# Turning values and phi(keys) to token layout by VectorE's 32x32 blocks and a DMA round trip instead of TensorE

## The chip, the cores and the metric

The kernel runs on one core of one Trainium2 chip. A core has a matrix engine (TensorE, PE in the profile, with its weight loads as PEld), a vector engine (VectorE, DVE), a scalar engine (ScalarE, ACT), GpSimd (POOL) and a sync engine (SyncE, SP) that here only issues DMAs. [...] The metric is the device time of one execution in microseconds; a comparison uses the median of several.

## The reference: one transformer block

The input x has 2048 tokens of 1024 features. The block computes h = x + A(layernorm(x)) and then h2 = h + B(layernorm(h)). B is an MLP: a dense layer to 3584 features, gelu, a dense layer back. A is attention with a compressive memory: 32 heads of 32 features; the tokens are taken in four segments of 512, and a memory M and a normaliser z are carried from one to the next:

```python
phi = lambda t: jnp.where(t > 0, t + 1.0, jnp.exp(t))
for s in range(N):
    logits = einsum("bhqd,bhkd->bhqk", qs, ks) * scale + mask
    a_dot = einsum("bhqk,bhkd->bhqd", softmax(logits), vs)
    a_mem = einsum("bhld,bhde->bhle", phi(qs), M) / (phi(qs) . z + 1e-6)
    outs.append(g * a_mem + (1 - g) * a_dot)
    M = M + einsum("bhld,bhle->bhde", phi(ks), vs)
    z = z + sum over tokens of phi(ks)
```

Two products sum over tokens: the attention product with vs and the memory update of phi(ks) with vs. TensorE sums over the partition axis, so both need vs (and the second phi(ks)) with tokens on partitions. All values are float32; the kernel splits each operand into an upper half that TensorE's fast format holds exactly and a lower half (the rest), and adds three products: upper-upper, upper-lower, lower-upper.

## The kernel before: units, slots and queues

The 2048 tokens are done in two halves of two segments each. In a half come the attention, the output projection (wo) and the MLP; the second half ends with the second MLP layer for all tokens. The change is in `attention`.

**Units.** Attention works on 8 groups of 4 heads (128 features) by 2 segments of the half: 16 units in a half, 32 in all. `dense(g, sl, ws, u)` (L402) makes a unit's operands: the projections of keys, queries and values in this order (`project`, 24 matmuls of 128x512 each, a yield after every third), into accumulators kps, qps, vps with features on partitions and 512 tokens along the row. Keys and queries are split (kh, kl, qh, ql) and copied by DMA into stacks of 96 partitions per head (`stack`, L372: twelve DMAs of 64 KB on SP's queue for the keys, twelve for the queries; five stack buffers for keys and five for queries). For segments 0 to 2, phi of the keys (pk) is made in the query projection's step 2 by `phi_sum`.

**Turning, before.** In step 1 of the value projection four TensorE transposes (L453) write pk in token layout to the accumulator pkn. ScalarE copies the upper half (pkh, L455), and in step 2 VectorE subtracts the lower (pkl, L457). After the value projection ScalarE copies vps to SBUF (vt, L461). The turn of the values is put off to the next unit: `late` (L466), a generator that the next unit's `dense` steps from the key projection's step 2 on. It issues four TensorE transposes (L469) to vn, the upper half by ScalarE (vs, L471) and the lower half by VectorE (L472). vs holds sixteen blocks of 64 columns (upper 32, lower 32), block 4 x (token block) + head. Then `late` queues the memory products (pm, segments 1 to 3: twelve matmuls) and the memory update (pmm, segments 0 to 2: twelve matmuls), which `one_small` hands out one by one between other TensorE work.

**Slots.** Beside the projections of a unit run the heads of the unit before (`heads`, `slot`): per head, scores (qk, L541), a maximum and exponential (L542, L550), a normalisation on GpSimd (L557), ten transposes of the weights (ptr, L573) with copies by ScalarE (pth, L575) and VectorE (ptl, L580), and the attention products with vs (av, L593), which come two head slots after the scores. `interleave` steps projections and slots in turn, six steps for a head, in the order PLAN (L31).

**What sets the order.** The text gives priorities; the framework plans each engine's and each DMA queue's order from them and from what it takes to be ready. Outside attention most of the text is pinned by `in_order`. An engine and a queue then run strictly in the planned order. Accumulators of tag "d" (three of 128x512) are shared by kps, qps, vps, pkn, vn, pm, pmm, pom and the output projection.

**The end of a half.** The last unit's heads run beside the first blocks of the output projection (`wo_first`, L729). Its fourth weight block lives in the tile pair that `zx_tile(x_, 3)` gives (tags th3 and tl3, one buffer each): `more` in L732.

Of the kernel before, what the change touches and what calls it, by code (L numbers as in the profile page):

```python
# [17 lines left out]
P = 128  # L18
# [25 lines left out]
def build(tc, x, wq, wk, wv, wo, beta, w1, b1, w2, b2, out):  # L44
# [6 lines left out]
    def ps_dense(name):  # L51
        return psum.tile([P, 512], F32, tag="d", name=name, bufs=3)
# [29 lines left out]
    p1_dram = [dram.tile([P, 512], F32, name=f"p1_dram{j}") for j in range(FB // 2)]  # L82
    h_dram = [[dram.tile([S // P, P, FB // 4, P], F32, name=f"h_dram{i}{s}") for s in range(2)] for i in range(2)]

    acts = {}

    def split(pool, w, hi, lo, hi_eng="vector", lo_eng="gpsimd"):
# [256 lines left out]
    def attention(half, first):  # L344
# [4 lines left out]
        def tmp(name):  # L349
            return ab.tile([P, 512], F32, tag="tmp", name=name, bufs=5)  # L350

        def tmpr(name):
            return ab.tile([P, 512], F32R, tag="tmpr", name=name, bufs=6)

# [12 lines left out]
        def phi_sum(parts, name, acc=None):  # L367
            o = tmp(name)
            nc.vector.scalar_tensor_tensor(o, parts[0], 1.0, parts[1], op0=ALU.min, op1=ALU.add, accum_out=acc)
            return o  # L370
# [31 lines left out]
        def dense(g, sl, ws, u):  # L402
# [15 lines left out]
            for c in project(ws["q"], sl, "qps", qps):  # L418
                if c == 0:
                    u["ks"] = stack(kh, kl, "ks", (0, 1, 0))  # L420
                if c == 2 and s < 3:
                    zc = ab.tile([P, 64], F32, name="zc", bufs=2)[:, 0:1]
                    pk = phi_sum(kparts, "pk", zc)
                next(behind, None)
                yield
            qh, ql = tmpr("qh"), tmpr("ql")
# [6 lines left out]
            for c in project(ws["v"], sl, "vps", vps):  # L433
                if c == 0:
                    u["qs"] = stack(qh, ql, "qs", (0, 0, 1))
                if s > 0:
                    if c == 2:
                        pq = phi_sum(qparts, "pq")
                    if c == 4:
                        while small:  # L440
                            one_small()
                        pqh, pql = tmpr("pqh"), tmpr("pql")
                        mzh = ab.tile([P, 256], F32R, name="mzh", bufs=1)[:, 0:132]
                        mzl = ab.tile([P, 256], F32R, name="mzl", bufs=1)[:, 0:132]
                        nc.scalar.copy(pqh, pq)
                        nc.gpsimd.tensor_copy(mzh, MZ[:, g, :])
                        nc.gpsimd.tensor_tensor(mzl, MZ[:, g, :], raw(mzh), op=ALU.subtract)
                    if c == 5:
                        nc.gpsimd.tensor_tensor(pql, pq, raw(pqh), op=ALU.subtract)
                if c == 1 and s < 3:  # L450
                    pkn = ps_dense("pkn")
                    for i in range(4):
                        nc.tensor.transpose(pkn[:, i * P:(i + 1) * P], pk[:, i * P:(i + 1) * P], ident)  # L453
                    pkh, pkl = tmpr("pkh"), tmpr("pkl")
                    nc.scalar.copy(pkh, pkn)  # L455
                if c == 2 and s < 3:
                    nc.vector.tensor_tensor(pkl, pkn, raw(pkh), op=ALU.subtract)  # L457
                next(behind, None)
                yield
            vt = tmp("vt")  # L460
            nc.scalar.copy(vt, vps)  # L461
            vs = ab.tile([P, 16, 64], F32R, name="vs", bufs=2)
            u["vs"] = vs
            omt = u["omt"] = tmp("omt") if s > 0 else None

            def late():  # L466
                vn = ps_dense("vn")
                for c in range(4):
                    nc.tensor.transpose(vn[:, c * P:(c + 1) * P], vt[:, c * P:(c + 1) * P], ident)  # L469
                vn3 = vn.rearrange("p (a b) -> p a b", b=DH)  # L470
                nc.scalar.copy(vs[:, :, 0:32], vn3)  # L471
                nc.vector.tensor_tensor(vs[:, :, 32:64], vn3, raw(vs[:, :, 0:32]), op=ALU.subtract)  # L472
                yield
                if s > 0:
                    om = tmp("om")
# [19 lines left out]
                if s < 3:  # L495
                    def update(pmm):
                        nc.vector.tensor_tensor(MZ[:, g, 0:P], pmm[:, 0:P], MZ[:, g, 0:P], op=ALU.add)  # L497
                        own = MZ[:, g, 0:P].rearrange("p (h e) -> p h e", h=4)
                        nc.gpsimd.tensor_tensor(own, own, hsel.unsqueeze(2).to_broadcast([P, 4, DH]), op=ALU.mult)
                        z = ZC[:, g:g + 1]  # L500
                        nc.gpsimd.tensor_scalar(z, z, zc, None, op0=ALU.add)
                        nc.gpsimd.tensor_scalar(MZ[:, g, 128:132], hsel, z, None, op0=ALU.mult)

                    smalls("pmm", [(lambda ps: ps[:, 0:P].rearrange("p (a b) -> p a b", a=4),
                                    pkh[:, c * P:(c + 1) * P], pkl[:, c * P:(c + 1) * P],
                                    vs[:, 4 * c:4 * c + 4, 0:32], vs[:, 4 * c:4 * c + 4, 32:64], c == 0, c == 3)
                                   for c in range(4)], update)
                total = len(small)
                while len(small) > total - left:
# [72 lines left out]
        def av(st, n):  # L582
# [3 lines left out]
            po = st["po"]  # L586
            for jk in (0, 1) if n == 0 else (3, 2):
                w = 512 - P * jk
                v = u["vs"][:, 4 * jk + j, :]
                for part in ("pth", "ptl"):  # L590
                    if (jk, part) != (3, "ptl"):
                        one_small()
# [851 lines left out]
```

## Time and profile before

| | us |
|---|---|
| timed runs, median of 3 | 2302.25 (2301.9 to 2303.4) |
| span of the profiled execution | 2296.2 |
| TensorE busy | 2270.4 |
| VectorE busy | 1540.3 |
| ScalarE busy | 1225.0 |
| GpSimd busy | 1092.4 |

The span runs from the first to the last instruction of one profiled execution; a timed run also holds what lies around it, so the two differ by some 6 us. Matmuls are pipelined: two that follow each other overlap in the records, and the distance between their starts tells what one costs. In the rows of the prediction "SPq" is an issue on SP's DMA queue, and a DMA row gives the median time from issue to landing. Row groups show busy time, the mean of one in ns, and the idle time of the engine just before them.

### The profile page before, as it was taken

What the parts mean: (1) busy time and instruction counts of PE and PEld (TensorE: products, weight loads), DVE (VectorE), ACT (ScalarE), POOL (GpSimd) and SP (SyncE); (2) the same over time, 40 slices, a digit from 0 to 9 for tenths busy, and PEclk for the clock granted to TensorE, in tenths of its full rate; (3) what the DMA queues carried; (4) which work ended last, traced back from release to release, by engine and by line L of the source; (5) the groups of instructions that cost most, each with busy time, mean ns of one, the idle gap of its engine ahead of it and who ended that gap; (6) DMA issues with size and microseconds to landing.
All of it is one profiled execution on the core that took longest, in us unless ns stands there. A gap on an engine that the chain in (4) does not pass through costs nothing.

```text
span 2296.2 us, 35279 instructions
## 1 busy us (share of the span) xinstructions
PE 2270.4 (99%) x11769; PEld 1890.8 (82%) x11769; DVE 1540.3 (67%) x3173; ACT 1225.0 (53%) x2549; POOL 1092.4 (48%) x1134
## 2 busy tenths in 40 slices
PE   8999999999999999999999999999999999999999
PEld 6888888878888888888888887888888888888887
DVE  6777777776655565777777777565566766577563
ACT  6777777775453445777777776363344223322221
POOL 5545555555244442555555556253445554155430
PEclk9999999999999999999999999999999999999999
DMA  6333333345465654433333344466667976476762
GB/s 190 92 85 91 93 89 85 87 120 182 139 204 172 188 165 142 113 91 86 85 87 88 87 111 140 156 211 175 176 188 263 345 243 216 159 253 221 249 234 90
DMA packets 322719, 355.36 MB, mean 155 GB/s; under 512 B 26190, under 2 KB 218730, under 8 KB 322538
## 3 DMA queue, kind: packets, MB, share of 16 engines
q1 hardware_dynamic: 259370, 316.40, 45.4%
q10 hardware_dynamic: 63168, 36.71, 5.3%
q8 instruction: 93, 1.52, 0.3%
q14 instruction: 88, 0.72, 0.1%
HBM read 226.59 MB, written 76.09 MB: 132 GB/s over the span
## 4 chain that ended last, share of the span: by engine, by line
PE 91%; ACT 3%; POOL 2%; DVE 2%; issue 1%; DMA 1%; ACTq 0%; SPq 0%; POOLq 0%; DVEq 0%
PE po L1278 22%; PE bps L882 9%; PE cps L882 7%; PE dps L882 6%; PE po L593 6%; PE ppt L573 6%; PE pqk L541 3%; PE vps L116 2%; PE vps L115 2%; PE kps L115 2%; PE kps L116 2%; PE vps L117 2%; PE kps L117 2%; PE pwo L117 2%; PE pwo L116 2%; PE pwo L115 2%
## 5 line engine op out<-in xcount | busy, mean ns | idle before, releaser
L557 POOL TENSOR_SCALAR pr<-pr,nm,gate 128x128 f32<-128x128 f32 (+3 forms) x512 | 322.6, 639 | 345.9 <-DVE nm L554 260.0
L550 ACT ACTIVATE pr<-pr,mx 128x256 f32<-128x256 f32 (+3 forms) x512 | 287.6, 562 | 161.9 <-DVE mx L542 158.2
L580 DVE TENSOR_TENSOR ptl<-ppt,pth 128x512 fp32r<-128x512 f32 (+1 forms) x384 | 227.2, 599 | 86.2 <-ACT pth L575 82.0
L542 DVE CUSTOM_DVE_ANT_0 pr<-pqk,mask 128x256 f32<-128x256 f32 (+3 forms) x512 | 243.3, 484 | 46.5 <-PE pqk L541 43.7
L573 PE MATMUL ppt<-ident,pr 128*128 128x128 f32 x1280 | 223.6, 277 | 2.1 <-POOL pr L557 1.4
L575 ACT CAST pth<-ppt 128x512 fp32r<-128x512 f32 (+1 forms) x384 | 194.2, 517 | 39.0 <-PE ppt L573 33.1
L1288 DVE TENSOR_TENSOR c<-c,po 128x512 f32<-128x512 f32 x160 | 105.4, 683 | 143.1 <-PE po L1278 135.5
L573 PEld LDWEIGHTS ppt<-ident,pr 128*128 128x128 f32 x1280 | 164.6, 140 | 32.5 <-POOL pr L557 2.6
L541 PE MATMUL pqk<-ks,qs 96*128 96x256 f32 (+3 forms) x512 | 161.3, 315 | 0.0
L92 POOL TENSOR_TENSOR wl<-wr,wh 128x1024 fp32r<-128x1024 f32 x52 | 124.5, 2393 | 70.8 <-PE pqk L541 27.6
L593 PE MATMUL po<-pth,vs 128*64 128x512 f32 (+3 forms) x512 | 155.4, 326 | 0.3 <-ACT pth L575 0.2
L593 PE MATMUL po<-ptl,vs 128*64 128x512 f32 (+3 forms) x512 | 153.9, 310 | 1.3 <-DVE ptl L580 1.2
L1278 PE MATMUL po<-w2h,zh 128*128 128x512 f32 x378 | 121.1, 390 | 0.8 <-DVE zh L1218 0.4
L1135 POOL TENSOR_TENSOR w2r<-w2r 128x512 f32<-128x512 f32 x54 | 85.4, 1593 | 72.0 <-DVE c L1288 36.9
L541 PEld LDWEIGHTS pqk<-ks,qs 96*128 96x128 f32 x512 | 96.2, 188 | 21.5
L994 POOL TENSOR_TENSOR s<-r 128x512 f32<-128x512 f32 x28 | 43.6, 1559 | 143.4 <-DVE sa L1010 87.1
L882 PE MATMUL bps<-zh,sb 128*128 128x512 f32 x336 | 111.0, 391 | 0.0
L882 PE MATMUL bps<-zh,sa 128*128 128x512 f32 x336 | 110.8, 390 | 0.0
L115 PE MATMUL vps<-yh,wh 128*128 128x512 f32 x256 | 109.4, 427 | 0.9 <-DVE MZ L497 0.9
L115 PE MATMUL kps<-yh,wh 128*128 128x512 f32 (+1 forms) x264 | 110.1, 417 | 0.0
L115 PE MATMUL qps<-yh,wh 128*128 128x512 f32 x256 | 106.8, 417 | 0.0
L1278 PE MATMUL po<-w2h,hl 128*128 128x512 f32 x322 | 103.2, 390 | 0.5 <-POOL hl L1218 0.3
(241 smaller groups left out, 6657.1 us busy)
## 6 DMA issues: line engine op xcount, KB each, us to landing
hr<-h_dram SPq DMA_DIRECT2D x112, 448.0 KB, 5.4
w2r<-in_B_w SPq DMA_DIRECT2D x122, 256.0 KB, 4.4
r<-in_B_w SPq DMA_DIRECT2D x56, 512.0 KB, 4.5
h_dram<-ht ACTq DMA_DIRECT2D x84, 256.0 KB, 3.7
ks<-kh SPq DMA_DIRECT2D x256, 64.0 KB, 2.0
qs<-qh SPq DMA_DIRECT2D x256, 64.0 KB, 2.0
wr<-in_A_wo SPq DMA_DIRECT2D x32, 512.0 KB, 4.0
wx<-in_B_w SPq DMA_DIRECT2D x56, 256.0 KB, 3.5
```

The costliest lines, as they stand in the source:

```text
L115: nc.tensor.matmul(ps, ah, bh, start=first, stop=False)
L116: nc.tensor.matmul(ps, ah, bl, start=False, stop=False)
L541: nc.tensor.matmul(pqk[:, :n], u["qs"][j][:, i * P:(i + 1) * P], u["ks"][j][:, 0:n], start=True, stop=True)
L542: nc.vector.tensor_tensor_reduce(out=st["pr"][:, offs[i]:offs[i] + n], in0=pqk[:, :n], in1=mask[:, 512 - n:512], op0=ALU.add, op1=ALU.min, ...
L550: nc.scalar.activation(pi, pi, AF.Exp, bias=mx[:, i:i + 1], scale=-1.0, accum_out=mx[:, 4 + i:5 + i])
L557: nc.gpsimd.tensor_scalar(pi, pi, nm[:, 4 + k:5 + k], gate[:, 1, 4 * g + j:4 * g + j + 1], op0=ALU.mult, op1=ALU.mult)
L573: nc.tensor.transpose(ppt[:, o:o + P], pr[:, offs[i] + jk * P:offs[i] + (jk + 1) * P], ident)
L575: acts["pth"] = n, nc.scalar.copy(pth[:, base:base + w], ppt[:, :w])
L580: nc.vector.tensor_tensor(o, x0, x1, op=ALU.subtract)
L593: nc.tensor.matmul(po[:, P * jk:], v, st[part][:, koff[jk]:koff[jk] + w], start=(jk, part) == (0, "pth"), stop=(jk, part) == (2, "ptl"))
L882: nc.tensor.matmul(ps, x_[:, c, :], y_[:, c, :], start=first and c == 0 and n == 0, stop=last and c == 3 and n == 2, skip_group_check=True)
L1278: nc.tensor.matmul(ps, x_[:, k], y_[k], start=opens and k == 0 and i == 0, stop=closes and k == self.KP - 1 and i == 2, skip_group_check=True)
```

## The change

A helper `turned(src, to, at)` turns a [128 features, 512 tokens] tile without TensorE. VectorE transposes 32x32 blocks into `mid`, with block columns reordered on the way; a DMA stores `mid` to DRAM; four DMAs read it back, each for one of four sets of 32 partitions, so that tokens lie on partitions. All five are issued by SP, and the reads follow the store. The result is ordered by head and then by token block, so the users' indices change (block 4 x head + token block). `turned` is called for pk in the query projection's step 3, and for vps, straight from the accumulator, at the end of the value projection; the copy vt, the eight transposes and the accumulators pkn and vn go. The upper halves are still copied by ScalarE, now from SBUF (that of the keys one step later), and the lower halves are subtracted by GpSimd instead of VectorE. `mid` and the result are quarters of two scratch tiles `scr` with the tags th3 and tl3, taken at the start of `attention`.

```diff
@@ -82,6 +82,7 @@
     p1_dram = [dram.tile([P, 512], F32, name=f"p1_dram{j}") for j in range(FB // 2)]
     h_dram = [[dram.tile([S // P, P, FB // 4, P], F32, name=f"h_dram{i}{s}") for s in range(2)] for i in range(2)]
 
+    turn_dram = [dram.tile([P, 512], F32, name=f"turn_dram{k}") for k in range(4)]
     acts = {}
 
     def split(pool, w, hi, lo, hi_eng="vector", lo_eng="gpsimd"):
@@ -349,6 +350,19 @@
         def tmp(name):
             return ab.tile([P, 512], F32, tag="tmp", name=name, bufs=5)
 
+        scr = [acts["zt"].tile([P, 4, 512], F32, tag=f"t{x_}3", name=f"sc{x_}") for x_ in "hl"]
+
+        def turned(src, to, at):
+
+            mid = at
+            nc.vector.transpose(mid.rearrange("p (c k d) -> p c k d", c=4, k=4), src.rearrange("p (k c d) -> p c k d", c=4, k=4))
+            d = turn_dram[acts.get("turned", 0) % len(turn_dram)]
+            acts["turned"] = acts.get("turned", 0) + 1
+            nc.sync.dma_start(d, mid)
+            for c in range(4):
+                nc.sync.dma_start(to[32 * c:32 * c + 32].rearrange("j (h x) -> j h x", h=4),
+                                  d[:, c * P:(c + 1) * P].rearrange("(h j) x -> j h x", h=4))
+
         def tmpr(name):
             return ab.tile([P, 512], F32R, tag="tmpr", name=name, bufs=6)
 
@@ -421,6 +435,9 @@
                 if c == 2 and s < 3:
                     zc = ab.tile([P, 64], F32, name="zc", bufs=2)[:, 0:1]
                     pk = phi_sum(kparts, "pk", zc)
+                if c == 3 and s < 3:
+                    kn = scr[1][:, 2 + sl]
+                    turned(pk, kn, scr[1][:, sl])
                 next(behind, None)
                 yield
             qh, ql = tmpr("qh"), tmpr("ql")
@@ -447,29 +464,26 @@
                         nc.gpsimd.tensor_tensor(mzl, MZ[:, g, :], raw(mzh), op=ALU.subtract)
                     if c == 5:
                         nc.gpsimd.tensor_tensor(pql, pq, raw(pqh), op=ALU.subtract)
-                if c == 1 and s < 3:
-                    pkn = ps_dense("pkn")
-                    for i in range(4):
-                        nc.tensor.transpose(pkn[:, i * P:(i + 1) * P], pk[:, i * P:(i + 1) * P], ident)
+                if c == 2 and s < 3:
                     pkh, pkl = tmpr("pkh"), tmpr("pkl")
-                    nc.scalar.copy(pkh, pkn)
-                if c == 2 and s < 3:
-                    nc.vector.tensor_tensor(pkl, pkn, raw(pkh), op=ALU.subtract)
+                    pkn = kn.rearrange("p (h k d) -> p k h d", h=4, k=4)
+                    pk4 = [x_.rearrange("p (k h d) -> p k h d", h=4, k=4) for x_ in (pkh, pkl)]
+                    nc.scalar.copy(pk4[0], pkn)
+                if c == 3 and s < 3:
+                    nc.gpsimd.tensor_tensor(pk4[1], pkn, raw(pk4[0]), op=ALU.subtract)
                 next(behind, None)
                 yield
-            vt = tmp("vt")
-            nc.scalar.copy(vt, vps)
+            vn = scr[0][:, 2 + sl]
+            turned(vps, vn, scr[0][:, sl])
             vs = ab.tile([P, 16, 64], F32R, name="vs", bufs=2)
             u["vs"] = vs
             omt = u["omt"] = tmp("omt") if s > 0 else None
 
             def late():
-                vn = ps_dense("vn")
-                for c in range(4):
-                    nc.tensor.transpose(vn[:, c * P:(c + 1) * P], vt[:, c * P:(c + 1) * P], ident)
                 vn3 = vn.rearrange("p (a b) -> p a b", b=DH)
                 nc.scalar.copy(vs[:, :, 0:32], vn3)
-                nc.vector.tensor_tensor(vs[:, :, 32:64], vn3, raw(vs[:, :, 0:32]), op=ALU.subtract)
+                nc.gpsimd.tensor_tensor(vs[:, :, 32:64], vn3, raw(vs[:, :, 0:32]), op=ALU.subtract)
+                vk = vs.rearrange("p (h k) e -> p k h e", h=4)
                 yield
                 if s > 0:
                     om = tmp("om")
@@ -503,7 +517,7 @@
 
                     smalls("pmm", [(lambda ps: ps[:, 0:P].rearrange("p (a b) -> p a b", a=4),
                                     pkh[:, c * P:(c + 1) * P], pkl[:, c * P:(c + 1) * P],
-                                    vs[:, 4 * c:4 * c + 4, 0:32], vs[:, 4 * c:4 * c + 4, 32:64], c == 0, c == 3)
+                                    vk[:, c, :, 0:32], vk[:, c, :, 32:64], c == 0, c == 3)
                                    for c in range(4)], update)
                 total = len(small)
                 while len(small) > total - left:
@@ -586,7 +600,7 @@
             po = st["po"]
             for jk in (0, 1) if n == 0 else (3, 2):
                 w = 512 - P * jk
-                v = u["vs"][:, 4 * jk + j, :]
+                v = u["vs"][:, 4 * j + jk, :]
                 for part in ("pth", "ptl"):
                     if (jk, part) != (3, "ptl"):
                         one_small()
```

## The prediction

> **What bounds the kernel now.** I read the page's head and its chain first, then the busy time of two attention stretches (the view by windows; only its sum row is shown), then TensorE in order of time.
>
> ```profile
> span 2296.2 us, 35279 instructions
> PE 2270.4 (99%) x11769; PEld 1890.8 (82%) x11769; DVE 1540.3 (67%) x3173; ACT 1225.0 (53%) x2549; POOL 1092.4 (48%) x1134
> PE 91%; ACT 3%; POOL 2%; DVE 2%; issue 1%; DMA 1%; ACTq 0%; SPq 0%; POOLq 0%; DVEq 0%
> sum 870.00, PE 866.72 PEld 732.20 DVE 653.16 ACT 637.50 POOL 469.87; mean PE 433.36 PEld 366.10 DVE 326.58 ACT 318.75 POOL 234.93
> ```
>
> TensorE carries 91% of the chain, and in the two attention stretches (870 us) it is busy 866.72 us, with VectorE at 75%, ScalarE at 73% and GpSimd at 54%. So TensorE time removed there shortens the kernel, as long as nothing new makes TensorE wait. How much a transpose costs is read from starts, not from durations:
>
> ```profile
> 213.46 0.39 PE L117 MATMUL vps<-yh,wl 128*128 128x512 f32 x1
> 213.69 0.60 PE L453 MATMUL pkn<-ident,pk 128*128 128x128 f32 x4
> 214.12 0.38 PE L573 MATMUL ppt<-ident,pr 128*128 128x128 f32 x2
> ...
> 217.41 0.34 PE L541 MATMUL pqk<-ks,qs 96*128 96x384 f32 x1
> 217.59 0.60 PE L573 MATMUL ppt<-ident,pr 128*128 128x128 f32 x4
> ...
> 220.91 0.39 PE L117 MATMUL vps<-yh,wl 128*128 128x512 f32 x1
> ...
> 224.44 0.60 PE L469 MATMUL vn<-ident,vt 128*128 128x128 f32 x4
> 224.79 0.43 PE L541 MATMUL pqk<-ks,qs 96*128 96x384 f32 x1
> 225.06 0.60 PE L573 MATMUL ppt<-ident,pr 128*128 128x128 f32 x4
> ...
> 227.48 0.22 PE L395 MATMUL pmm<-vs,pkh 128*128 128x128 f32 x1
> ```
>
> Columns: start, duration, engine. Four key transposes hold the next work back by 214.12 - 213.69 = 0.43 us. Four value transposes take 224.79 - 224.44 = 0.35 us, and the score matmul behind them needs 0.27 us to its successor instead of the 0.18 us at 217.41: together 0.44 us.
>
> **The change, part by part.** Counts and durations by line:
>
> ```profile
> L453 PE MATMUL pkn<-ident,pk 128*128 128x128 f32 x96 | 14.4, 272 | 0.0
> L469 PE MATMUL vn<-ident,vt 128*128 128x128 f32 x128 | 19.3, 273 | 0.6 <-ACT vt L461 0.6
> L461 ACT COPY vt<-vps 128x512 f32<-128x512 f32 x32 | 18.9, 592 | 1.0 <-PE vps L117 0.9
> L472 DVE TENSOR_TENSOR vs<-vn,vs 128x512 fp32r<-128x512 f32 x32 | 22.0, 686 | 0.7 <-ACT vs L471 0.4 <-DMA qs<-qh 0.3
> L369 DVE SCALAR_TENSOR_TENSOR pk<-e,r 128x512 f32<-128x512 f32 x24 | 21.5, 894 | 20.4 <-ACT r L364 20.4
> L449 POOL TENSOR_TENSOR pql<-pq,pqh 128x512 fp32r<-128x512 f32 x24 | 31.0, 1290 | 27.4 <-ACT pqh L445 26.1 <-DMA qs<-ql 1.3
> ```
>
> *TensorE removed:* 24 key turns (96 / 4) x 0.43 us and 32 value turns (128 / 4) x 0.44 us = 10.3 + 14.1 = **24.4 us**. This is the gain's ceiling.
>
> [...]
>
> *ScalarE:* the copy of L461 goes (18.9 us in all, not on the path, counted as nothing). The upper halves of L455 and L471 stay, now read from on-chip memory instead of the accumulators.
>
> *VectorE:* 56 subtractions go (L472 and its twin L457, 0.69 us each) and 56 block transposes of 128x512 come. No row shows such a transpose. A one-pass 128x512 operation costs between the 0.69 us of L472 and the 0.89 us of L369; I take 0.69 and a balance of nothing. At 0.89 it would be 11 us more over an engine that is idle a quarter of the time, hidden. If it were half as fast as that, some 40 us; still hidden in sum, but late by 0.7 us each time.
>
> *GpSimd:* 56 subtractions of 128x512 at the 1.29 us of L449 = 72 us more, 1.3 us per turn. In the two stretches it is idle 400 of 870 us, so the sum is covered; the place in its queue is the third rival.
>
> *DMAs:* each turn adds five issues to SP's queue, a 256 KB store and, behind a wait for its landing, four 64 KB reads. The rows for them and for SP's queue now:
>
> ```profile
> ks<-kh SPq DMA_DIRECT2D x256, 64.0 KB, 2.0
> o_dram<-ot SPq DMA_DIRECT2D x28, 256.0 KB, 2.3
> orr<-o_dram SPq DMA_DIRECT2D x28, 256.0 KB, 3.2
> ```
> ```profile
> 220.89 0.59 SPq L377 DMA_DIRECT2D qs<-ql  x1
> 231.99 0.51 SPq L377 DMA_DIRECT2D ks<-kh  x1
> ```
> ```profile
> 237.65 0.59 SPq L377 DMA_DIRECT2D ks<-kh  x1
> ...
> 243.83 1.17 SPq L377 DMA_DIRECT2D qs<-qh  x2
> ...
> 250.74 0.59 SPq L377 DMA_DIRECT2D qs<-ql  x1
> ```
> ```profile
> 233.84 0.70 DVE L369 SCALAR_TENSOR_TENSOR pk<-e,r 128x512 f32<-128x512 f32 x1 [1.08 <-ACT r L364]
> ```
> ```profile
> 251.98 0.28 PE L541 MATMUL pqk<-ks,qs 96*128 96x256 f32 x1
> ```
>
> An issue takes 0.63 us: twelve stack loads from 243.83 to 250.74. A turn therefore holds SP for about 0.35 + 2.3 (landing) + 4 x 0.63 = 5.2 us. There is room where it falls: after a unit's last stack load (220.89) SP has nothing until 231.99, and the values are ready at 221.3. The keys of the next unit are ready at 233.84 + 0.70 = 234.5; SP is at the stack loads until 237.65 + 0.59 = 238.24, and 5.6 us lie between that and the query stacks at 243.83, part of them taken by other loads.
>
> *When the turned values arrive.* The last value matmul ends at 220.91 + 0.39 = 221.30. Block transpose 0.69: 222.0. Store landed 2.3 later: 224.3. The fourth read is issued 1.9 later, at 226.2, and lands 2.0 to 3.2 later: 228.2 to 229.4. Upper half on ScalarE 0.59, lower on GpSimd 1.29: **230.1 to 231.3**. Before:
>
> ```profile
> 225.08 0.59 ACT L471 CAST vs<-vn 128x512 fp32r<-128x512 f32 x1 [0.83 <-PE vn L469]
> ```
> ```profile
> 225.74 0.69 DVE L472 TENSOR_TENSOR vs<-vn,vs 128x512 fp32r<-128x512 f32 x1
> ```
>
> so both halves stood at 226.43, some 4 to 5 us sooner. The first user now is the memory update (pmm) at 227.48. That holds for the eight units of segment 0. In segments 1 and 2 twelve memory products are queued ahead of the update, and the attention products of these values come two heads later (L593 is issued two head slots behind L541). So in eight units the update would be 3 to 4 us late where it stands. I count 0.25 us for each (2 us, between 0 and 8 x 3.8 = 30), since an engine's order is not that of the text but one planned by readiness:
>
> ```profile
> 212.70 0.59 ACT L427 CAST qh<-qps 128x512 fp32r<-128x512 f32 x1
> 213.19 0.72 ACT L550 ACTIVATE pr<-pr,mx 128x512 f32<-128x512 f32 x1
> ```
>
> Here the copy of the queries went ahead of an exponential that the text puts first. The planner can move the update behind projections in the same way, if it knows how long the round trip takes.
>
> *End of each half.* The scratch is the tile in which the output projection keeps its fourth weight block; its split now waits for the last values' lower half.
>
> ```profile
> 500.62 0.39 PE L117 MATMUL vps<-yh,wl 128*128 128x512 f32 x1
> ```
> ```profile
> 509.64 1.05 ACT L91 CAST zh<-wr 128x1024 fp32r<-128x1024 f32 x1
> ```
> ```profile
> 502.09 12.54 SPq L700 DMA_DIRECT2D wr<-in_A_wo  x4
> ```
>
> The values end at 501.0, so by the same chain (8.8 to 10.0 us) the tile is free at 509.8 to 511.0 against the present start at 509.64. I take 2 us for each half, 4 in all; 0 if other work fills it, 24 if the turn queues behind the loads that hold SP for 12.5 us.
>
> Sum: 24.4 - 2 - 4 = 18.4 us less. The profiled span 2296.2 becomes 2277.8; the timed median, 2302.25, has 6.05 us around that span, so **2284 us**.
>
> **Rivals.**
>
> *Slower: ScalarE and GpSimd stand waiting for the round trip.* If the copy L471 keeps a place near 225.08, it waits until 228.2 to 229.4, 3.1 to 4.3 us, with exponentials and the copies that feed the attention products queued behind it in order, and TensorE waiting for those. It decides against the change once TensorE loses more than 24.4 / 32 = 0.76 us per unit. Price: 3.7 us x 32 = 118 us if all of it comes through; ScalarE's 27% idle time and the two heads in flight absorb part. With half, 59 - 24.4 + 4 = 39 us slower, 2341. For it: the chain is long, and it falls on the engine with the most consumers. Against it: ordering by readiness, and the keys have 9 us before they are used.
>
> *No gain: GpSimd's queue.* A lower half goes ahead of the normalisation that feeds the transposes of the weights.
>
> ```profile
> 221.35 1.41 POOL L557 TENSOR_SCALAR pr<-pr,nm,gate 128x384 f32<-128x384 f32 x2 [2.77 <-DVE nm L554]
> ```
> ```profile
> 513.14 2.38 POOL L557 TENSOR_SCALAR pr<-pr,nm,gate 128x384 f32<-128x384 f32 x2
> ```
> ```profile
> 512.37 1.86 DVE L92 TENSOR_TENSOR zl<-wr,zh 128x1024 fp32r<-128x1024 f32 x1
> ```
>
> A normalisation ended at 222.76 for transposes at 225.06: 2.3 us of room, enough for 1.29. But beside a VectorE subtraction of two on-chip tiles the same pair took 2.38 instead of 1.41 us. With both stretched, 1.29 x 1.69 + 0.97 = 3.15, 0.85 us over the room; if half of the 56 meet that, 24 us, and with the 6 us above the time is 2308; with a quarter, 2296. I write 2302. [...]
>
> *Less gain: SP's queue.* The keys' round trip fits into the 5.6 us gap if nothing else does; if none of it is hidden, the query stacks start 5.2 us later. The first stack's three loads are out at 245.7, landed at 247.7, and used at 251.98, 4.3 us of room. So TensorE loses up to 0.9 us in at most the 24 units that turn keys, 22 us; I put half, 11 us: 2295.
>
> [...]
>
> **How the numbers follow.** Two runs of this kernel can be told apart by about 0.2%, 4.6 us. Chances: forecast 0.45 (2276 to 2297), waiting engines 0.32 (2305 to 2400), GpSimd 0.13 (2296 to 2308), SP 0.07 (2284 to 2306), full durations 0.03. Faster: 0.45 + 0.03 + 0.05 (SP, part) = 0.53. Same: 0.08 + 0.02 = 0.10. Slower: 0.32 + 0.05 = 0.37. The range runs from 2274, 4 us under the ceiling with nothing lost (2302 - 24.4 = 2278), to 2341, where half of the first rival is left out (0.16) beside the 0.03 below. The forecast's own range is 2276 to 2297.
>
> **What would show it.** Right: L453 and L469 gone from TensorE, the unit shorter by 0.87 us (0.44 in segment 3), no ScalarE wait on the read DMAs, TensorE's idle time still under 30 us. Wrong: in the waits, ScalarE's upper halves or GpSimd's lower halves waiting for the read-back, with TensorE waiting for pth or ptl behind them; block transposes well over 0.9 us; stack loads landing after their score matmul is due. If the planner puts the round trip's users where they stand now, the forecast fails.

## The result and the profile after

The changed kernel takes 2385.27 us (median of 4 runs, 2381.67 to 2387.80); beside it the kernel before took 2302.07. The ratio is 1.0362 (95% interval 1.0347 to 1.0376): **83 us slower**, where 2284 was forecast and 2341 was the end of the range. The profiled execution took 2383.45 us.

The page's head, and the view by windows over the same two attention stretches, first of the changed kernel, then of the kernel before. The columns of a window are its length, the busy time of PE, PEld, DVE, ACT and POOL, the granted TensorE clock, the DMA share and GB/s.

```profile
span 2381.7 us, 35312 instructions
...
PE 2295.9 (96%) x11545; PEld 1901.2 (80%) x11545; DVE 1543.6 (65%) x3173; ACT 1202.8 (51%) x2517; POOL 1165.1 (49%) x1190
```
```profile
60.00:490.00 430.00, 399.67 (x2218) 331.85 (x2217) 282.67 (x826) 265.88 (x683) 235.71 (x305) 0.94 0.43 113
930.00:1370.00 440.00, 419.99 (x2404) 352.52 (x2403) 309.31 (x885) 289.14 (x718) 245.56 (x317) 0.97 0.44 116
sum 870.00, PE 819.65 PEld 684.37 DVE 591.98 ACT 555.02 POOL 481.26; mean PE 409.83 PEld 342.19 DVE 295.99 ACT 277.51 POOL 240.63
```
```profile
60.00:490.00 430.00, 428.87 (x2610) 362.45 (x2610) 320.11 (x947) 312.26 (x793) 221.17 (x313) 1.00 0.35 89
930.00:1370.00 440.00, 437.85 (x2665) 369.74 (x2663) 333.05 (x990) 325.24 (x821) 248.70 (x330) 1.00 0.35 90
```

Two things are new. TensorE, which was busy 866.72 of these 870 us, is now busy 819.65: it stands 50 us. And its granted clock, 1.00 before, is 0.94 and 0.97. Over the whole span it is 0.981:

```profile
core 0: 2381.7 us, clock 0.981
```

So 0.019 x 2381.7 = 45 us' worth of clock is missing too. By the clock records of the trace 92 us of the span run at half the clock, and TensorE works in 84 of them, so some 42 us of the loss are clock. No other engine is near its limit: VectorE, the next busiest, works 592 of the 870 us.

Over the whole span TensorE is idle 2381.7 - 2295.9 = 85.8 us, where it was idle 2296.2 - 2270.4 = 25.8. These 60 us more and the 42 of clock, less some 19 that the missing transposes are worth (see no_wait below), make the 83.

How long is a unit? Take the last value product of the same two units, eight units apart, in each half (rows of TensorE in order of time; first the kernel before, then the changed one):

```profile
468.51 0.39 PE L117 MATMUL vps<-yh,wl 128*128 128x512 f32 x1
...
1032.19 0.39 PE L117 MATMUL vps<-yh,wl 128*128 128x512 f32 x1
...
1278.56 0.39 PE L117 MATMUL vps<-yh,wl 128*128 128x512 f32 x1
```
```profile
248.46 0.39 PE L118 MATMUL vps<-yh,wl 128*128 128x512 f32 x1
...
521.04 0.39 PE L118 MATMUL vps<-yh,wl 128*128 128x512 f32 x1
...
1113.39 0.39 PE L118 MATMUL vps<-yh,wl 128*128 128x512 f32 x1
...
1362.99 0.39 PE L118 MATMUL vps<-yh,wl 128*128 128x512 f32 x1
```

Before, (468.51 - 220.91) / 8 = 30.95 us in the first half (the row at 220.91 stands in the prediction) and (1278.56 - 1032.19) / 8 = 30.80 in the second. After, (521.04 - 248.46) / 8 = **34.07** and (1362.99 - 1113.39) / 8 = **31.20**. The first half loses 3.1 us per unit, where 0.87 were to be gained; the second does not gain. By the ends of the units, the changed kernel is 55 us behind at the end of the first half's units, 81 us behind from the fifth unit of the second half on, and 85 at the end. So the loss has three places: 21 us by the end of unit 4 (its last value product is at 147.97 instead of 127.06), 34 us in the twelve units behind them, and 26 us between the end of the first half's units and the fifth unit of the second half.

**Where TensorE stands.** The waits of TensorE between 100 and 500 us (total, times, longest), and one unit of segment 0 in order of time:

```profile
PE pmm L409 <- POOL vs L485: 14.2, 7, 2.6
PE pmm L409 <- ACT r L378: 7.3, 4, 2.2
...
```
```profile
317.74 0.39 PE L118 MATMUL vps<-yh,wl 128*128 128x512 f32 x1
318.17 0.72 DVE L358 STREAM_TRANSPOSE sch<-vps 128x512 f32<-128x512 f32 x1
...
319.80 0.53 SPq L361 DMA_DIRECT2D turn_dram<-sch  x1
...
322.07 1.87 SPq L363 DMA_DIRECT2D sch<-turn_dram  x4
...
327.67 2.37 POOL L93 TENSOR_TENSOR wl<-wr,wh 128x1024 fp32r<-128x1024 f32 x1 [1.04 <-PE po L607]
327.92 0.61 ACT L484 CAST vs<-sch 128x512 fp32r<-128x512 f32 x1
...
330.00 1.75 POOL L485 TENSOR_TENSOR vs<-sch,vs 128x512 fp32r<-128x512 f32 x1
...
331.80 0.33 PE L409 MATMUL pmm<-vs,pkh 128*128 128x128 f32 x1 [2.61 <-POOL vs L485]
```

The last value product ends at 318.13. Block transpose, store and reads follow as forecast, the store 0.9 us late behind a stack load; the lower half then queues behind a weight split on GpSimd and ends at 331.75, 13.6 us after the products. The update was due 2.61 us sooner.

In segment 1 the read-back itself is later, and ScalarE with it. The four reads land a median of 5.2 us after their issue, where they took 2.2 in the unit of segment 0 above; two weight loads of 512 KB stand just ahead of them on SP's queue. (The DMA rows below are of the reads of segment 0, then of segment 1 with the second weight load: KB each, median us from issue to landing.) ScalarE stands 1.16 us for the read-back, with the keys' exponential and Relu queued behind; the update needs the keys' accumulator, so it waits for that Relu (GpSimd's lower half, 364.63 + 1.26, ends at the same moment):

```profile
sch<-turn_dram SPq DMA_DIRECT2D x4, 64.0 KB, 2.2
```
```profile
wr<-in_A_wq SPq DMA_DIRECT2D x1, 512.0 KB, 5.9
sch<-turn_dram SPq DMA_DIRECT2D x4, 64.0 KB, 5.2
```
```profile
354.93 0.40 SPq L327 DMA_DIRECT2D wr<-in_A_wk  x1
356.89 0.38 SPq L327 DMA_DIRECT2D wr<-in_A_wq  x1
357.37 2.04 SPq L363 DMA_DIRECT2D sch<-turn_dram  x4
...
363.93 0.62 ACT L484 CAST vs<-sch 128x512 fp32r<-128x512 f32 x1 [1.16 <-DMA sch<-turn_dram]
364.63 1.26 POOL L485 TENSOR_TENSOR vs<-sch,vs 128x512 fp32r<-128x512 f32 x1 [3.73 <-ACT vs L484]
364.85 0.57 ACT L377 ACTIVATE e<-kps 128x512 f32<-128x512 f32 x1
365.32 0.58 ACT L378 ACTIVATE r<-kps 128x512 f32<-128x512 f32 x1
...
365.96 0.33 PE L409 MATMUL pmm<-vs,pkh 128*128 128x128 f32 x1 [1.90 <-ACT r L378]
```

**What the stand does to the clock.** The same place by windows of 3.4 us:

```profile
329.50:332.90 3.40, 1.10 (x10) 1.10 (x10) 1.99 (x4) 1.46 (x4) 3.40 (x5) 1.00 0.49 124
332.90:336.30 3.40, 3.40 (x14) 2.81 (x13) 0.97 (x2) 0.57 (x1) 1.56 (x6) 0.52 0.72 197
336.30:339.70 3.40, 3.40 (x20) 2.82 (x19) 1.75 (x5) 1.76 (x4) 2.64 (x3) 0.98 0.36 96
```

After the window with 1.10 us of work comes one at half the clock, full of work: 14 matmuls in it, 20 in the next. The 128x512 products start 0.43 us apart in it (334.91, 335.34 and 335.77), where they start 0.23 us apart in the kernel before (226.78, 227.01 and 227.25). By its granted clock such a window costs an estimated 1.7 us (half of 3.4), nearly as much as the stand. That accounts for the unit of the first half from the seventh unit on: a stand of (2.61 + 1.90) / 2 = 2.26, plus 1.7 of clock, less 0.87 for the transposes, is 3.1 us, as measured.

It does not account for units 2 to 4. There (38 to 148 us) the view of waits lists 9.6 us for TensorE, of which 3.7 are at the update; the rest are at the weight transposes, at a projection that waits for a weight split, and at two score products. The clock is halved for 24 us, which is some 11 us lost.

### The profile page after: what moved, and what is told of

Its sections match the earlier page's. It is cut to its first block, busy times and chain, and to the rows that moved or that the text cites. A ratio compares the mean times of both kernels' runs of the same rounds, so it can differ in the third digit from the quotient of the medians.

```text
span 2381.7 us, 35312 instructions
## 1 busy us (share of the span) xinstructions
PE 2295.9 (96%) x11545; PEld 1901.2 (80%) x11545; DVE 1543.6 (65%) x3173; ACT 1202.8 (51%) x2517; POOL 1165.1 (49%) x1190
## 4 chain that ended last, share of the span: by engine, by line
PE 79%; POOL 5%; ACT 4%; DMA 4%; DVE 4%; issue 3%; SPq 2%; POOLq 0%; ACTq 0%; DVEq 0%
PE po L1292 22%; PE bps L896 10%; PE cps L896 6%; PE dps L896 6%; PE po L607 4%; PE ppt L587 4%; DMA sch<-turn_dram 3%; PE pwo L117 2%; PE pwo L118 2%; PE pwo L116 2%; POOL wl L93 2%; PE qps L117 2%; PE qps L118 2%; PE qps L116 2%; PE pqk L555 2%
## 5 line engine op out<-in xcount | busy, mean ns | idle before, releaser
L116 PE MATMUL qps<-yh,wh 128*128 128x512 f32 x256 | 113.3, 443 | 0.0
L118 PE MATMUL qps<-yh,wl 128*128 128x512 f32 x256 | 107.2, 419 | 1.6 <-POOL wl L93 1.6
```

The costliest lines, as they stand in the source:

```text
L116: nc.tensor.matmul(ps, ah, bh, start=first, stop=False)
L118: acts["mm"] = nc.tensor.matmul(ps, al, bh, start=False, stop=last)
```

## The experiments

Theory A: TensorE stands because the turned values come later than the place that the order gives their users, by latency alone. Rival B: GpSimd's added work. Rival C: SP's queue. Rival D: the keys' turn. Each run gives a median and its ratio to the kernel before on the same chip, with the 95% interval.

**The update later (pmm_later)**

```diff
                 left = len(small)
                 if s < 3:
+                    for _ in range((8, 8, 0)[s]):
+                        yield
+                    left = min(left, len(small))
```

> The changed kernel with the memory update's products (pmm) given out eight steps of the unit later in segments 0 and 1, so that they stand 14.2 to 15.4 us of TensorE work behind the last value product instead of 10.5 to 12.1. Theory A (TensorE stands at the update because the turned values' lower half lands 12 to 14 us behind the last value product, and each stand is followed by 3.4 us at half the granted clock): the stands of 1.6 to 2.6 us in units 1 to 15 and their slow windows go; what stays is the change of half (+18 us) and the second half; 2308 us, 2295 to 2320. Rival B (GpSimd's slower lower halves are too much for its queue): the stands move to other instructions that wait for GpSimd, over 2360. Rival C (the round trip holds SP's queue, so that stack loads come late): the stands move to the score products, over 2360.

2345.58 us, ratio 1.0185 (1.0170 to 1.0200). Half of the loss goes, not nearly all, and the time lies in none of the forecast ranges. The unit of the first half falls from 34.07 to 30.97 us and the stands at the update all but vanish (0.8 us is left), as A says; but it does not fall below the 30.95 of before. The waits of the same stretch show what took their place:

```profile
PE ppt L590 <- POOL pr L574: 8.5, 14, 1.4
...
```

The rest sits in the first five units (14 us) and at the change of half (22 us).

**Lower halves on VectorE (low_dve)**

```diff
-                nc.gpsimd.tensor_tensor(vs[:, :, 32:64], vn3, raw(vs[:, :, 0:32]), op=ALU.subtract)
+                nc.vector.tensor_tensor(vs[:, :, 32:64], vn3, raw(vs[:, :, 0:32]), op=ALU.subtract)
```

(and the same for pkl)

> The changed kernel with both lower halves back on VectorE (0.7 us each instead of 1.36, and not behind GpSimd's weight splits). Theory A: the update's operand lands some 2.4 us sooner in segment 0 and 0.7 us sooner in segment 1, so the first kind of stand (2.6 us) goes nearly and the second (1.9 us) stays at about 1.2, with its slow window; half of the loss of the first half comes back: 2350 us, 2335 to 2365. Rival B (GpSimd's queue): nearly all comes back, under 2300. Rival C (SP's queue or the round trip alone): under 10 us come back, over 2375.

2349.69 us, 1.0212 (1.0193 to 1.0230), as A forecast. Between 100 and 500 us the waits of pmm for VectorE's lower half are 5.6 us (longest 1.0) in place of 14.2 for GpSimd's; those for the Relu stay (9.5).

**Keys alone, values alone**: the other one turned as in the kernel before.

> The keys turned as in the changed kernel, the values by TensorE with VectorE's lower half as before. Theory A: the values stand in time for the update, no stand; the keys' gain of 24 x 0.43 = 10 us shows: 2292 us, 2287 to 2302. Rival D (it is the keys' round trip, 56% of the SP time in the middle of the stack loads, that does the harm): over 2330.

2304.84 us, 1.0011 (1.0002 to 1.0021). No stand in the units, so D falls; but not the 10 us of gain either. It is 1.1 us ahead at the end of the first half's units, and loses 6 us in one place at the start of the second, where the memory products wait 2.9 us for GpSimd's lower half of the queries and the clock is halved for 6.8 us behind.

keys_dve is keys_alone with that kind of work taken from GpSimd: the keys' lower half goes to VectorE.

> keys_alone with the keys' lower half on VectorE. In keys_alone GpSimd's lower half stood ahead of the lower half of the queries at the start of the second half, TensorE stood 2.88 us and had half the clock for 6.8 us; without them 6 us less: 2299 us, 2295 to 2303, the first of these kernels at or under the time before. If GpSimd's place in the queue is not the cause: 2304 to 2306.

2303.83 us, 1.0013 (1.0004 to 1.0022). The memory products still wait 2.6 us for the queries' lower half at the start of the second half; GpSimd's subtraction for the keys was not the cause. In the trace ScalarE takes the queries' upper half at 917.65, behind its copy of the keys from the read-back, where the kernel before took it at 909.86; on GpSimd a weight split of 2.80 us then goes ahead of the lower half. Why the planned order puts it there stays open.

> The values turned as in the changed kernel, the keys by TensorE with VectorE's lower half as before. Theory A: all the stands stay, and the keys' 10 us of TensorE come back on top: 2385 to 2400 us, or some us less where GpSimd is freer. Rival B: with half of GpSimd's added work gone (32 of 75 us), half of the loss goes: about 2345. Rival D: under 2310.

2367.15 us, 1.0291 (1.0264 to 1.0318). All stands of the first half are there (15.8 us for the lower half and 10.6 for the Relu, 100 to 500 us), so the values do it. The time is under what A forecast: the 18 us less than the full change come at the change of half, which I had not foreseen.

**What are the transposes worth? (no_turn, no_turn_fit)** In the kernel before:

```diff
-                    pkn = ps_dense("pkn")
-                    for i in range(4):
-                        nc.tensor.transpose(pkn[:, i * P:(i + 1) * P], pk[:, i * P:(i + 1) * P], ident)
+                    pkn = pk
...
-                vn = ps_dense("vn")
-                for c in range(4):
-                    nc.tensor.transpose(vn[:, c * P:(c + 1) * P], vt[:, c * P:(c + 1) * P], ident)
-                vn3 = vn.rearrange("p (a b) -> p a b", b=DH)
+                vn3 = vt.rearrange("p (a b) -> p a b", b=DH)
```

> The kernel before with the 224 transposes of keys and values left out and nothing in their place: the halves are made straight from the unturned tiles, so that part of the computation is missing. It shows what TensorE's removed work is worth with no round trip, no block transpose and no GpSimd work. Theory E (the ceiling of the prediction stands, all 24.4 us, and the round trip alone eats them): 2278 us, 2274 to 2283. Theory F (TensorE at 99% hides waits with next to no room, above all its weight transposes behind GpSimd's normalisation, and these take most of what the transposes leave): 2288 to 2302.

2297.36 us, 0.9977 (0.9968 to 0.9987): 5 us, not 24. TensorE's freed time turns into a stand once in two units, at the update, for a Relu that reads the keys' accumulator. no_turn_fit moves that user, and the one of the second half, later:

> no_turn (the transposes of keys and values left out of the kernel before, nothing in their place) with two users moved: the memory update of segment 1 six steps later, the transposes of the read memory one step later in the second half. In no_turn TensorE stands 1.08 us at that update once in two units of the first half, for ScalarE's Relu that still reads the keys' accumulator, and 0.88 us at the read memory in the second half. Theory H (these two places alone keep the 24.4 us from showing; the order has to follow the removed work): about 6 x 1.08 + 6 x 0.88 + what follows on them, 2283 to 2289 us. Theory F (many waits have next to no room, the next one takes it): 2292 to 2299, like no_turn.

2298.28 us, 0.9990 (0.9981 to 0.9999). The stand has only moved. The waits of TensorE from 100 to 500 us, no_turn first:

```profile
PE pmm L395 <- ACT r L364: 6.5, 6, 1.1
```
```profile
PE pom L516 <- DVE om L479: 6.8, 6, 1.1
```

**Both edits, and the read memory later (both, fit_a)**: fit_a adds two yields ahead of `pom` in the second half.

> The two edits of pmm_later and low_dve together: the update eight steps later in segments 0 and 1, and the lower halves on VectorE. Theory A (the stands at the update) and B (GpSimd's queue) as two separate causes add up: pmm_later kept 14 us of loss in units 1 to 4 and 22 us at the change of half, low_dve removed 18 us around the change of half; together 2315 us, 2303 to 2330. If one of the two makes the other needless: 2345.

> As both, and in the second half the transposes of the read memory (pom) two steps later, since TensorE stands there 1.2 to 2.0 us once in two units for VectorE's second half of om. If those stands are what eats the second half's gain of 0.4 to 0.9 us per unit: 8 us under both. If another wait has as little room: the same as both within 3 us.

both: 2342.77 us, 1.0173 (1.0157 to 1.0190). The two gains don't add up, as the second forecast said: as in pmm_later, the weight transposes wait for GpSimd's normalisation (10.2 us in twelve waits from 100 to 500 us, against 8.5). fit_a: 2329.52, 1.0120 (1.0105 to 1.0135); 13 us less, all of them in the second half, whose unit is 30.59 us against 31.13 in both.

**The same work, no wait for the round trip (no_wait)**

```diff
                     turned(pk, kn, scr[1][:, sl])
+                    kn = scr[1][:, sl]
...
             turned(vps, vn, scr[0][:, sl])
+            vn = scr[0][:, sl]
```

> The changed kernel with all its work (block transposes, stores, reads back, GpSimd's lower halves), but the halves are made from the block-transposed tile itself, which is there before the round trip: the gathering of the blocks is left out of the result, and nothing waits for the DMAs' data. Theory A (what costs is the latency of the round trip, for which the order leaves too little): near no_turn, which does the same with VectorE's lower halves: 2295 to 2310 us. Rival B (the added work on GpSimd): over 2325. Rival C (SP's queue is held by the store and the four reads, the stack loads come late): over 2325, with stands at the score products.

**2294.74 us, 0.9971 (0.9959 to 0.9982).** With every block transpose, store, read and GpSimd subtraction still in place it is 90 us faster than the changed kernel and 6 faster than before. So B and C fall as added work: all they can cost here is within the 13 us that this kernel stays behind the 19 which its units gain (below). As a part of the latency both stay: GpSimd's subtraction, slower than VectorE's (a mean of 1.36 us against 0.69) and, in the unit of segment 0 above, behind a weight split of 2.37 us, is worth 36 us (low_dve), and in segment 1 the reads land behind weight loads on SP's queue (5.2 us from issue to landing); no run takes these loads out of the way, so their share is not shown. Its units, and the only wait of TensorE that the view lists from 100 to 500 us:

```profile
221.82 0.39 PE L118 MATMUL vps<-yh,wl 128*128 128x512 f32 x1
...
463.85 0.39 PE L118 MATMUL vps<-yh,wl 128*128 128x512 f32 x1
...
1032.75 0.39 PE L118 MATMUL vps<-yh,wl 128*128 128x512 f32 x1
...
1275.10 0.39 PE L118 MATMUL vps<-yh,wl 128*128 128x512 f32 x1
```
```profile
PE po L609 <- DVE ot L620: 1.5, 1, 1.5
```

(463.85 - 221.82) / 8 = 30.25 and (1275.10 - 1032.75) / 8 = 30.29 us: 0.70 and 0.51 less than before, some four fifths of the 0.87 and 0.65 that the prediction's figures give. Why it does better than no_turn was not tested by itself; what differs is that the copy vt is gone from ScalarE and the subtractions from VectorE, and the update's wait for the Relu is gone with them. The total gains only 6 us since TensorE stands in three other places (2.7 us in the third unit, 2.2 at the start of the second half, and at its end), with slow windows behind: the mean granted clock of the profiled execution is 0.996. One reservation: the order of this kernel was planned for the early halves, so it shows the latency together with what the planner makes of it.

**Can the order cover the latency? (fit_b, mix_a to mix_e)** fit_b is fit_a with the values' halves two steps later as well, and the update seven and six steps behind them instead of eight.

> As fit_a (update later, lower halves on VectorE, read memory later in the second half), and the upper and lower halves of the values are given out two steps later too, so that ScalarE and VectorE, which in fit_a still stand 9.0 us for the read-back and 15.6 us for the upper halves behind it, find it landed. If these stands are what is left of the loss (27 us in fit_a): 2305 to 2315 us. If the loss that is left comes from the order that the late halves force on the other work (halves between scores and exponentials, the start of each half): 2320 to 2335.

2322.90 us, 1.0087 (1.0071 to 1.0104): better, but over the lower forecast.

The mixed kernels keep GpSimd's lower halves and turn by TensorE where `rt` is false; where it is true, the halves come `a` steps later and the update `b` and `c` (2, 7, 6 in mix_a; 3, 6, 6 in mix_b; 0, 8, 8 in mix_c), and the read memory one step later in the second half:

```diff
+            rt = u["rt"] = g >= 1
...
+                if rt:
+                    vn = vn0
+                    for _ in range(a):
+                        yield
...
+                    for _ in range((b, c, 0)[s] if rt else 0):
+                        yield
```

> The change as it is (GpSimd's lower halves too), but: the first block of heads in each half keeps the transposes on TensorE; behind it the values' halves are given out two steps later, the memory update seven and six steps later (segments 0 and 1), the read memory one step later in the second half. Without a wait for the round trip a unit was 0.70 us (first half) and 0.51 us (second half) shorter than before, and the losses sat in the first units of each half. Theory A (the loss is latency, and the order can be made to cover it): a unit of 30.3 to 30.7 us, the whole 2285 to 2300 us. Rival I (whatever is put later is missed by the next user, so latency can only be moved): units of 31.0 us or more as in pmm_later and fit_b, 2305 to 2325.

> As mix_a, with the values' halves three steps later instead of two (the update six steps behind them in both segments, 16 to 17 us of TensorE work behind the last value product). Theory A: the same as mix_a or better, where ScalarE and GpSimd still stood for the read-back in mix_a; 2285 to 2300. Rival I: later still, the attention products of the same values wait; over mix_a by 5 us or more.

> As mix_a, with the values' halves where the change has them (no step later) and only the update later (eight steps), so that ScalarE and GpSimd stand waiting for the read-back ahead of other work. What it is over mix_a is the price of these engines standing (the slower rival of the prediction by itself): 8 us or more if that stand reaches TensorE, within 3 us if it is covered.

mix_a 2310.94 us, 1.0038 (1.0023 to 1.0053); mix_b 2308.79, 1.0030 (1.0021 to 1.0040); mix_c 2304.38, 1.0013 (1.0003 to 1.0022). mix_a and mix_b miss A's 2300. mix_a lies in Rival I's range, though its unit (30.90 us in the first half, 30.71 in the second) stays under Rival I's 31.0; mix_b is 2 us under mix_a, where Rival I had it 5 us over. Even so, the first block of each half on TensorE, the later update and, in the second half, the later read memory together take back 80 of the 83 us. mix_c, whose ScalarE and GpSimd do stand for the read-back, is the fastest of the three, against my expectation: those stands alone cost nothing that shows here. What is left of mix_c's loss sits at the end of the first half, where TensorE stands 2.7 us for a lower half of the weights (ptl) and has half the clock behind:

```profile
509.00:512.40 3.40, 1.57 (x8) 0.85 (x7) 3.07 (x11) 3.01 (x9) 2.34 (x3) 1.00 0.91 258
512.60:516.00 3.40, 3.05 (x11) 2.76 (x12) 2.45 (x8) 0.00 (x0) 2.95 (x4) 0.52 0.00 0
```

mix_d takes each half's last block out too (`rt = 1 <= g < NG - 1`), mix_e the whole first half instead (`rt = half == 1 and g >= 1`).

> As mix_c, with the last block of heads of each half on TensorE's transposes too, so that nothing of the round trip meets the output projection's first weights. In mix_c 8 us were lost between the last values of the first half and the first of the second (rows of the unit ends: 1.3 us behind the kernel before, then 9.3). Theory A: these go: 2297 us, 2294 to 2300. If the place at the end of the half is not the cause: 2302 to 2306, as mix_c.

> As mix_c, with the round trip in the second half alone, blocks 2 to 8 of heads. There mix_c's unit was 30.45 us against 30.80 before, with no stand over 0.75 us. Theory A: 14 units x 0.35 = 5 us less than before: 2297 us, 2295 to 2300. If the gain is given back at the end of the half: 2300 to 2303.

**mix_d: 2297.13 us, 0.9978 (0.9967 to 0.9988); mix_e: 2299.57, 0.9985 (0.9976 to 0.9994).** Both lie in A's range. mix_d is 5 us faster than the kernel before and 88 faster than the changed one. The gain is the second half's: there mix_d's unit is (1275.52 - 1033.57) / 8 = 30.24 us against 30.80, but in the first half it is (469.89 - 220.43) / 8 = 31.18 against 30.95. Its granted clock is 1.000, and its page reads:

```profile
span 2294.8 us, 35288 instructions
...
PE 2254.7 (98%) x11601; PEld 1873.9 (82%) x11601; DVE 1535.5 (67%) x3173; ACT 1209.5 (53%) x2525; POOL 1161.8 (51%) x1176
```

## Why the prediction was wrong, point by point

*The step that failed* is the late memory update: "In eight units the update would be 3 to 4 us late where it stands. I count 0.25 us for each (2 us, between 0 and 8 x 3.8 = 30)". The lateness was seen; the belief that the planner would move the update behind it was wrong. Where 2 us were counted, TensorE stands 20.7 + 8.3 + 3.5 = 32.5 us at the update, and behind ten of the eleven stands of 1.5 us or more the clock is halved:

```profile
PE pmm L409 <- POOL vs L485: 20.7, 11, 3.0
PE pmm L409 <- ACT r L378: 8.3, 5, 2.2
PE pmm L409 <- ACT vs L484: 3.5, 5, 1.1
```

The planner did move the update: TensorE was ready for it at 331.80 - 2.61 = 329.19, 11.1 us behind the last value product, where before the update came after 6.2 (227.48 - 221.30). But the data came after 13.6. Put eight steps later, the update stands 0.8 us in all from 100 to 500 us (pmm_later).

*"In segments 1 and 2 twelve memory products are queued ahead of the update"*: counted as safe, it was not. In segment 1 the update stood 1.6 to 2.2 us, through the accumulator that it takes over from the keys and a ScalarE that waits for the read-back.

*The start of a half* has no term in the sum. By the end of unit 4 it costs 21 us; in mix_c, which keeps the first block of heads on TensorE, the fourth unit ends 0.8 us behind the kernel before. Which of the waits there starts the loss was not tested.

*The arrival chain*: 8.8 to 10.0 us after the products was forecast, 13.6 measured. Block transpose (0.70 us each against 0.69), the store's landing and the issues were right. The reads' landing, 2.0 to 3.2 us in the forecast, was right in the unit of segment 0 (2.2) and not in that of segment 1 (5.2), where weight loads go ahead. Left out were also the waits for a free SP and for ScalarE's turn (the third read had landed at 325.06, the copy starts at 327.92), and GpSimd's own queue: a weight split of 2.37 us ahead, and 1.75 us for the subtraction, where the median of the 32 is 1.29; VectorE was busy in 1.72 of these 1.75 us, and whether that made it longer was not tested.

```profile
L485 POOL TENSOR_TENSOR vs<-sch,vs 128x512 fp32r<-128x512 f32 x32 | 43.5, 1360 | 43.2 <-ACT vs L484 43.2
L473 POOL TENSOR_TENSOR pkl<-scl,pkh 128x512 fp32r<-128x512 f32 x24 | 31.8, 1324 | 11.3 <-ACT pkh L471 11.3
L358 DVE STREAM_TRANSPOSE sch<-vps 128x512 f32<-128x512 f32 x32 | 22.5, 704 | 1.7 <-PE vps L118 1.2
```

*The ceiling, 24.4 us*: the starts were read rightly. Where nothing waits (no_wait) units gain 0.70 and 0.51 us, 16 x 0.70 + 16 x 0.51 = 19 us, against 0.87 and 0.65 forecast. But the condition "as long as nothing new makes TensorE wait" was hard to meet: no_turn gains 5 us, since waits just behind TensorE's had almost no room.

*VectorE, GpSimd and SP as loads*: costed at nothing and rightly so; GpSimd's 75 us of added work (43.5 + 31.8) are all in no_wait. The rivals of GpSimd's queue and of SP's queue were wrong in their mechanisms (over the whole run TensorE waits 2.3 us for normalisations at the weight transposes, and the view lists no wait for a stack load); both queues matter as latency of the turned values (low_dve, 36 us; the reads of segment 1).

*The end of each half*: 4 us for two. The change of half costs 26 us, the first units of the second half included; mix_c, which keeps the first two of those on TensorE, still loses 8 us at the end of the first half that mix_d does not.

*The slower rival* (chance 0.32, 2341 with half coming through) was the case. Its price of 118 us for all of it, less the 24.4, plus the 4, would have been 2400; 2385 was measured. That the two are near is luck: the price holds no clock, and its mechanism was not quite the one written. The wait that hurt most was TensorE's own at the update, not ScalarE's in front of pth and ptl.

*Left out altogether*: the clock. A stand could cost not its length but its length and 1.7 us more for each slow window behind it, of which there were one to three; some 42 us of the loss are clock.

## What to carry to other kernels

When work leaves a bottleneck engine for a path with a longer latency, list the first user of the result and its distance in time, and add to the latency every queue that the new chain passes; the order must be moved by hand if the planner's idea of the latency is short. An engine at 99% hides waits that have no room, so a removed microsecond may show as another engine's wait (here no_turn gained 5 of 24 us): run a kernel with the work simply left out before pricing its removal. And keep such a path away from the edges of a stage: here the start of the first half and the change of half lost 21 + 26 = 47 of the 83 us.

## What the runs showed of the hardware that I had not expected

The clock reacted to short stands. I took the matmul starts of all eighteen traces, in each window of 3.41 us between 60 and 515 and between 900 and 1400 us that was itself at full clock (the clock records of the traces give the windows' length and edges: in the changed kernel the slow stretches last 3.41, 6.83 or 10.24 us, and the full ones between them 2 to 117 times 3.41), and added up how much longer the distances between starts were than the median for the same kind of matmul. All 34 windows with more than 2.3 us of idle time counted so were followed by one at half the clock; of 4833 with 1.8 us or less only two were; of the 53 between these, 27 were. The view by windows, which counts busy time, gives 3.40 - 1.10 = 2.30 us of idle time for the window at 329.50 above, which was followed by half the clock, and 3.40 - 1.95 = 1.45 for this one of mix_d, which was not:

```profile
1017.50:1020.90 3.40, 1.95 (x12) 1.51 (x11) 3.34 (x11) 2.54 (x6) 2.31 (x7) 1.00 0.38 116
1020.90:1024.30 3.40, 3.40 (x22) 2.76 (x21) 2.13 (x10) 2.07 (x7) 3.33 (x5) 1.00 0.42 130
```

So here a stand cost a window or nothing, by how much of it fell into one window. In the changed kernel the 2.61 us ahead of 331.80 cost one, and most of them lay in one window. The 1.67 us ahead of 297.50 lay in one window (1.73 us of work in the 3.40 from 295.50), and the next had a clock of 0.50; the 1.63 us ahead of 1030.13 fell into two (2.50 us of work in the 3.40 from 1026.00, 2.67 in the 3.40 from 1029.40), and the clock stayed at 1.00 in the one behind them. For this kernel some 2 us in one window could be enough.
